# Attention and two expert layers on one core: the attention of a pair of heads written in two halves, with TensorE's instructions inside a half kept in the written order

## The chip, the core and the metric

The kernel runs on one core of a Trainium2 chip. The metric is device time in microseconds (us) for one launch, the median of several runs. Engines are named as in the profile: PE is TensorE's matmul stream, PEld its weight loads, DVE is VectorE, ACT is ScalarE, POOL is GpSimd, SP issues most DMAs.

## What is computed

Banded attention with four sink columns, then a dense gated layer, then a routed layer with one of eight experts per token, all in float32:

```python
# attention: 4 batches, 8 heads, 768 positions, head size 64, window 128, 4 sinks
scores = scale * np.matmul(q, k.transpose(0, 1, 3, 2))
keep = (pos[None, :] < n_sink) | ((rel >= 0) & (rel < window))
scores = np.where(keep, scores, -1e9); scores -= scores.max(-1, keepdims=True)
a = np.exp(scores); a = a / (a.sum(-1, keepdims=True) + 1e-9)
x = (a @ v).transpose(0, 2, 1, 3).reshape(3072, 512)
# dense layer: 512 -> 1024 (gated) -> 1024 -> 512
x = ((x @ w1) * (x @ w2)) @ w3 @ w_out
# routing and expert layer: 512 -> 1024 -> 512, one expert a token
logits = x @ w_gate + modality_bias[modality_id]
e_idx = argmax(logits); gate = softmax(logits)[e_idx]
out = gate * (relu(x @ e_w1[e_idx]) @ e_w2[e_idx])
```

## The kernel before

Precision comes from splitting: a float32 operand is held as a high and a low part, and a product is three matmuls (high by high, high by low, low by high). The weight product w3 @ w_out is formed once at the start (tiles `w3o`).

The tokens are cut into 12 units of 256 queries. One step of attention is a **pair** n: one unit and two heads, so there are 48 pairs, four to a unit. `att_stream` (L574) is a generator that traces the pairs; a pair is built of these functions:

- `a_scores(n, j)` (L441), for the two query blocks j = 0, 1: six matmuls at L458 into the tile `sp`, 64 rows of the array each (one head in the upper half, one in the lower). Then on DVE the mask (L470 or L475) and the row maximum (L484), on ACT the two exponentials (L486). `sp` has one buffer, so the scores of j = 1 wait for the exponentials of j = 0, and those of the next pair for the exponentials of j = 1. The normalisation on DVE (L491, L492, L497) is put off to a later step by `defer`.
- `a_pt(n)` (L518): four transposes of the probabilities at L527 into `pt`, a copy on ACT (L531), two masked copies on POOL (L536).
- `a_skT(n)` (L502): one or two transposes of the sink columns (L509).
- `a_pv(n)` (L541): the product with v at L555, 64 columns of the array each (one head left, one right), and the sinks' part at L558, then the split of the result into `xb` (L561 on ACT, L566 on DVE). The listing of the program shows four or six matmuls at L555 a pair; the trace has two records for each.
- `a_tqk(n)` (L389): from pair 8 on, the transposition of q and k on DVE (L407) and their split on ACT and DVE (L414 to L428).

The pairs are software pipelined: the step for pair n traces the scores of pair n, the transposes and the product with v of pair n - 1, and q and k of pair n + 1. `front` (L1014) mixes attention with the dense layer. For each of six groups of two units it runs `moe1_stream` (L687) and, between its pieces, as many steps of attention as a linear due time asks for (L1102, L1104). The dense layer of a group is eight pairs of products `ab` (L724, 24 matmuls of 512 columns per f), which DVE and ACT turn into `g`, `gh` and `gl` (L728 to L734, L701, L702), and the products `x2p` (L712) with `w3o`: first those of the first unit, mixed with `ab`, then, in the "late" part, those of the second unit alone. `route` (L775) follows: 16 multiply-and-sum instructions a unit on DVE (L785), a small ranking on PE (L807 to L811, tile `rk`), and the tables. `back` (L1126) then runs the expert layer (L933, L970).

What stands in the instruction queues is not the traced order. When the program is built, a scheduler reorders each engine's instructions: it goes through time by its own estimates and lets an engine take, of the instructions that it holds to be ready, the one with the best priority, which is the trace's order unless the code says otherwise. On the chip each engine's queue then runs strictly in the order so fixed, with semaphores between engines.

Of the kernel before, what the change touches and what calls it, by code (L numbers as in the profile page):

```python
# [27 lines left out]
def attention_moe_moe_kernel(ctx, tc, q, k, v, w1, w2, w3, w_out, mod_id, w_gate, mod_bias, e_w1, e_w2, out,  # L28
# [57 lines left out]
    def tick():  # L86
        for fn in waiting[0]:
            fn()
        waiting[0], waiting[1] = waiting[1], []

    def settle():
        while waiting[0] or waiting[1]:
# [253 lines left out]
    def a_load(n):  # L346
        u, p = divmod(n, NP)
        b, c = divmod(u, NC)
        hs = slice(2 * p, 2 * p + 2)
        qk = att.tile([128, 2, UNIT], F32, tag="qk", bufs=2, name="qk")  # L350
        for x, src in enumerate((q, k)):
            if n < BY_PE:
                for j in range(2):
                    s0 = c * UNIT + j * 128
                    nc.sync.dma_start(out=qk[:, x, j * 128:(j + 1) * 128].rearrange("p (h d) -> p h d", h=2),
                                      in_=src[b, hs, s0:s0 + 128, :].rearrange("h s d -> s h d"))
                continue
            for g in range(4):
                h, d0 = 2 * p + g // 2, g % 2 * 32
                nc.sync.dma_start(out=qk[g * 32:(g + 1) * 32, x].rearrange("p (b i) -> p b i", i=32),  # L360
                                  in_=src[b, h, c * UNIT:(c + 1) * UNIT, d0:d0 + 32].rearrange("(b s) i -> s b i", s=32))
        nat[n] = qk

    def a_load_v(n):
        u, p = divmod(n, NP)
        b, c = divmod(u, NC)
        hs = slice(2 * p, 2 * p + 2)
        vn = att.tile([128, 3, 2, D], F32, tag="vn", bufs=3, name="vn")
        for j in range(0 if c else 1, 3):
            s0 = c * UNIT + (j - 1) * 128  # L370
            nc.sync.dma_start(out=vn[:, j], in_=v[b, hs, s0:s0 + 128, :].rearrange("h s d -> s h d"))
        stt["v", n] = vn
        if n and c == 0 and p == 0:
            a_load_sinks(b)
# [143 lines left out]
    def a_pt(n):  # L518
        u, p = divmod(n, NP)
        b, c = divmod(u, NC)  # L520
        P = stt["p", n]
        for j in range(2):
            stt.pop(("norm", n, j))()
        tp = ps_t.tile([128, 4, 128], F32, tag="t", name="pt")
        for j in range(2):
            for h in range(2):
                nc.tensor.transpose(out=tp[:, 2 * j + h, :], in_=P[:, j, h * (KW + NS):h * (KW + NS) + 128], identity=idf)  # L527
        full = att.tile([128, 4, 128], F32, tag="ptf", bufs=1, name="ptf")
        parts = att.tile([128, 2, 2, 2, 128], F32, tag="ptp", bufs=1, name="ptp")
        i0 = 0 if c else 1  # L530
        nc.scalar.activation(out=full[:, 2 * i0:4], in_=tp[:, 2 * i0:4], func=ACTF.Copy)  # L531
        if i0:
            nc.scalar.activation(out=parts[:, 0, 0], in_=tp[:, 0:2], func=ACTF.Copy)
        for a, op in enumerate((ALU.is_ge, ALU.is_gt)):
            sign = 1 - 2 * a
            nc.gpsimd.affine_select(out=parts[:, a, i0:2].rearrange("p j h q -> p (j h) q"), in_=full[:, 2 * i0:4],  # L536
                                    pattern=[[0, 4 - 2 * i0], [sign, 128]], compare_op=op, fill=0.0, base=0,
                                    channel_multiplier=-sign)
        stt["pt", n] = parts
# [34 lines left out]
    def att_stream():  # L574
        a_tqk(0); yield
        a_load(1)
        a_load_sinks(0)
        a_vsink(0)
        yield
        for n in range(NN):  # L580
            if n + 2 < NN:
                a_load(n + 2)
            a_scores(n, 0); yield
            if n:
                a_load_v(n)
                a_pt(n - 1); a_skT(n - 1); yield
            if n + 1 < NN:
                a_tqk(n + 1)
            yield
            a_scores(n, 1); yield  # L590
            if n:
                a_pv(n - 1)
                att_done[0] = n
                if n % (NP * NC) == 0:
                    a_vsink(n // (NP * NC))
            yield
        a_pt(NN - 1); a_skT(NN - 1); yield
        a_pv(NN - 1)
        att_done[0] = NN
        yield  # L600
# [412 lines left out]

    def front():  # L1014
        att_it = att_stream() if banded else att_stream_full()
        steps = [0]

        def step_att():
            if next(att_it, 0) == 0:
                return False  # L1020
            steps[0] += 1
            tick()
            return True

        def att_upto(target):
            while steps[0] < target and step_att():
                pass

        unit_steps = ATT_STEPS * NP
        begun = 10 if banded else 4  # L1030
        wab_n = W_EARLY
        t = 0.0
        f64_ahead(2)
        if banded:
            a_load(0)
            a_load_v(0)
        f64_ahead(4)
        for i, c in enumerate(startup_stream()):
            t += c
            tick()  # L1040
            if att_done[0] < 2 * NP:
                att_upto(min(0.75 * (i + 1), 8) + 38 * t / 46700)
        early = []
        for gr in range(NU // 2):
            while att_done[0] < (2 * gr + 2) * NP:
                step_att()
            settle()
            last = gr == NU // 2 - 1
            if last:
                for _ in att_it:  # L1050
                    pass
                att_ctx.close()
                pool = p2a.enter_context(tc.tile_pool(name="p2a", bufs=1, side="right", reuse_waits="tile"))
                mem = mem_of(pool, wp, pool, pool, pool, pool, (ps_t, ps_ab, ps_x2, 1))
                p2a_pool.append(pool)
                mem["w1"] = halves(lambda: pool.tile([128, 1024], F32R, tag="w1", bufs=KD, name="w1"), mem["w"])
                rows0 = pool.tile([128, SLOT // 128, ROW], F32, name="xrows")
                t_banks = [mem["pt"], lambda: ps_x.tile([128, 512], F32, tag="x", name="x")]

                def next_bank():  # L1060
                    t_banks.reverse()
                    return t_banks[0]()

                mem["pt"] = next_bank

                def next_early(first=0):
                    slots.append(Slot(SLOT, (NU - 2 if slots else NU - 4) * UNIT, mem))
                    slots[-1].decide(first)

                def first_early():  # L1070
                    next_early(3)
                    slots[0].gather(rows0)

                first_early()
                early = [(10000 + 2000 * i, lambda i=i: slots[0].w1_piece(i)) for i in range(KD)]
                early += [(47000 + 1500 * i, next_early) for i in range(N_EARLY - 1)]
                early += [(57200 + 1300 * i, lambda i=i: slots[0].transposes(i)) for i in range(KD)]
            t, routed, s0 = 0.0, 0, steps[0]
            s1 = begun + (2 * gr + 3) * unit_steps
            for kind, c in moe1_stream(gr):  # L1080
                t += c
                tick()
                while gr == 0 and wab_n < KF and wab_n < W_EARLY + t / 4000:
                    wab_pair(wab_n)
                    wab_n += 1
                    if wab_n == KF:
                        wgate_by_expert()
                        start_ctx.close()
                        sp_[0] = m1_ctx.enter_context(tc.tile_pool(name="m1", bufs=1, reuse_waits="tile"))
                        consts_late()  # L1090
                        load_wgate()
                if last:
                    while early and t >= early[0][0]:
                        early.pop(0)[1]()
                    due = min(t, 46000) / 1100
                else:
                    due = min(t, 46000) / 1100
                while routed < due and kind != "late":
                    routed += 1
                    route_step()  # L1100
                if kind != "late":
                    att_upto(min(s0 + (s1 - s0) * t / 52000, s1))  # L1102
                else:
                    att_upto(s1 + unit_steps * (t - 52000) / 10400)  # L1104
            for _, fn in early:
                fn()
        settle()
# [131 lines left out]
```

## Time and profile before

| | |
|---|---|
| median of 3 runs | 975.77 us (975.64 to 976.39) |
| the profiled execution | 975.55 us |
| its span, first to last instruction | 973.8 us |
| PE busy | 932.9 us, 96% |
| DVE busy | 651.8 us, 67% |
| ACT busy | 440.5 us, 45% |
| POOL busy | 167.2 us, 17% |
| mean granted PE clock | 0.994 |

A busy time is the sum of the stretches in which an engine had an instruction in execution; consecutive matmuls overlap in the record (a 512-column matmul lasts about 0.39 us there and the next one starts 0.23 us after it), so what a matmul costs is read from the distance of two starts. A busy PE is not a PE at its best pace. The rows further down come from the views named above each of them.

### The profile page before, as it was taken

Reading aid. Unit: us, or ns where it says so; the run is one execution under the profiler, and the core shown is the slowest. Engines: PE = TensorE matmul, PEld = TensorE weight load, DVE = VectorE, ACT = ScalarE, POOL = GpSimd, SP = SyncE. Lnnn points to the kernel's source line nnn. Section 1 sums busy time; section 2 is a strip of 40 time slices with the busy share of each in tenths; the row PEclk is TensorE's granted clock in tenths of the full one; section 3 lists DMA queues with packets and bytes.
Section 4 is the critical chain, followed back from the end, with each engine's and each line's share of the span. In section 5 each row is a group of like instructions: output and inputs, shape, how many; then the busy total and the mean of one; then the engine's idle time right before and its main releaser. Section 6 shows DMA issues by size and latency. Waiting matters only on the chain. (4 is left out here: it accounts for less than half of the span.)

```text
span 973.8 us, 15418 instructions
## 1 busy us (share of the span) xinstructions
PE 932.9 (96%) x4840; PEld 709.7 (73%) x4840; DVE 651.8 (67%) x1953; ACT 440.5 (45%) x1218; POOL 167.2 (17%) x253
## 2 busy tenths in 40 slices
PE   4899999999999999999999999999999999999995
PEld 3567677767776777677767776887888888888883
DVE  7956996699659964896599649929934374333422
ACT  3687763454335433553365334314433443344433
POOL 1111121111112111211111112213021214111010
PEclk9999999999999999999999999999999999999998
DMA  8754754123212231236123200512446465443331
GB/s 258 237 149 122 210 121 127 34 53 71 51 23 48 61 56 20 52 71 44 23 53 67 56 9 9 178 40 87 139 164 129 153 69 191 132 149 120 109 134 41
DMA packets 168933, 94.02 MB, mean 97 GB/s; under 512 B 140231, under 2 KB 148679, under 8 KB 168720
## 3 DMA queue, kind: packets, MB, share of 16 engines
q1 hardware_dynamic: 164080, 80.13, 33.6%
q0 software_dynamic: 4768, 12.88, 4.1%
q8 instruction: 39, 0.64, 0.3%
q14 instruction: 46, 0.38, 0.2%
HBM read 80.14 MB, written 13.09 MB: 96 GB/s over the span
## 5 line engine op out<-in xcount | busy, mean ns | idle before, releaser
L724 PE MATMUL ab<-xb,wab 128*128 128x512 f32 x1152 | 288.7, 397 | 1.0 <-DVE g L734 1.0
L724 PEld LDWEIGHTS ab<-xb,wab 128*128 128x128 f32 x1152 | 209.7, 188 | 46.0 <-PE sp L458 1.1
L970 PE MATMUL x<-w 128*128 128x512 f32 x600 | 141.0, 392 | 0.0
L785 DVE CUSTOM_DVE_ANT_0 junk<-rows,wgb 128x512 bf16<-128x512 f32 x192 | 135.7, 707 | 2.0 <-ACT rows L772 0.9
L712 PE MATMUL x2p<-w3o,gh 128*128 128x512 f32 x384 | 128.9, 411 | 0.5 <-ACT gh L701 0.5
L970 PEld LDWEIGHTS x<-w 128*128 128x128 f32 x600 | 111.6, 188 | 23.1 <-DVE w L202 0.4
L536 POOL TENSOR_SCALAR_AFFINE_SELECT ptp<-ptf 128x512 f32<-128x512 f32 (+1 forms) x96 | 66.5, 716 | 308.0 <-ACT ptf L531 308.0
L701 ACT ACTIVATE gh<-g 128x256 fp32r<-128x256 f32 x96 | 39.9, 416 | 119.2 <-DVE g L731 98.6
L486 ACT ACTIVATE P<-sp,st 128x132 f32<-128x132 f32 (+1 forms) x192 | 69.2, 366 | 51.5 <-DVE st L484 45.8
L712 PEld LDWEIGHTS x2p<-w3o,gh 128*128 128x128 f32 x384 | 67.2, 188 | 18.0 <-ACT gh L701 2.9
L202 DVE TENSOR_TENSOR w<-wst,w 128x512 fp32r<-128x512 f32 x112 | 71.4, 685 | 10.5 <-ACT w L201 10.5
L937 DVE SCALAR_TENSOR_TENSOR w<-ab,w 128x512 fp32r<-128x512 f32 x48 | 33.1, 690 | 64.4 <-ACT w L936 64.2
L712 PE MATMUL x2p<-w3o,gl 128*128 128x512 f32 x192 | 76.0, 396 | 0.0
L933 PE MATMUL ab<-w,w 128*128 128x512 f32 x288 | 74.9, 395 | 0.0
L933 PE MATMUL ab<-w 128*128 128x512 f32 x288 | 73.6, 391 | 0.0
L201 ACT ACTIVATE w<-wst 128x512 fp32r<-128x512 f32 x112 | 63.4, 628 | 4.5 <-DMA wst<-in_moe_w_dram 4.5
L458 PE MATMUL sp<-ring,qh 64*128 64x264 f32 (+1 forms) x384 | 61.1, 329 | 3.2 <-ACT P L486 2.2
L458 PEld LDWEIGHTS sp<-ring,qh 64*128 64x128 f32 x384 | 37.0, 185 | 35.8 <-ACT P L486 15.5
L933 PEld LDWEIGHTS ab<-w,w 128*128 128x128 f32 x288 | 53.9, 188 | 12.4
L933 PEld LDWEIGHTS ab<-w 128*128 128x128 f32 x288 | 54.1, 188 | 12.1
L936 ACT ACTIVATE w<-ab 128x512 fp32r<-128x512 f32 x48 | 28.7, 597 | 71.8 <-PE ab L933 71.4
L974 POOL DMA_INDIRECT out_dram<-late,ti x25 | 25.2, 1009 | 203.9 <-ACT late L973 166.6
(201 smaller groups left out, 1392.9 us busy)
## 6 DMA issues: line engine op xcount, KB each, us to landing
wst<-in_moe_w_dram SPq DMA_DIRECT2D x56, 512.0 KB
f64st<-in_moe_w_dram SPq DMA_DIRECT2D x32, 512.0 KB
vn<-in_v_dram SPq DMA_DIRECT2D x128, 64.0 KB
xs<-rows SPq DMA_DIRECT2D x12, 513.0 KB
qk<-in_q_dram SPq DMA_DIRECT2D x160, 32.0 KB
qk<-in_k_dram SPq DMA_DIRECT2D x160, 32.0 KB
f64st<-in_moe_w_out_dram SPq DMA_DIRECT2D x8, 512.0 KB
wgb<-wgt SPq DMA_DIRECT2D x1, 2048.0 KB
```

What stands on the lines that cost most here:

```text
L201: nc.scalar.activation(out=hi, in_=src, func=ACTF.Copy)
L202: lo_eng.tensor_tensor(out=lo, in0=src, in1=f32(hi), op=ALU.subtract)
L458: nc.tensor.matmul(out=sp[:, h, c0:c0 + nk].rearrange("p (a b) -> p a b", b=KW), lhsT=a[hp, j, :], rhs=kr[hp, b_, blocks, c0:c0 + KW], sta ...
L486: nc.scalar.activation(out=rows[:, h], in_=seen[:, h], func=ACTF.Exp, bias=st[:, 0, h:h + 1], accum_out=st[:, 1, h:h + 1])
L536: nc.gpsimd.affine_select(out=parts[:, a, i0:2].rearrange("p j h q -> p (j h) q"), in_=full[:, 2 * i0:4], pattern=[[0, 4 - 2 * i0], [sign, ...
L701: nc.scalar.activation(out=gh, in_=g, func=ACTF.Copy)
L712: nc.tensor.matmul(out=x2p[t], lhsT=a[:, sl], rhs=b_, start=(f == 0 and i == 0), stop=(f == KF - 1 and i == 2))
L724: nc.tensor.matmul(out=bank[nm].rearrange("p (u t) -> p u t", u=2), lhsT=a, rhs=b_, start=(kk == 0 and i == 0), stop=(kk == KD - 1 and i = ...
L785: nc.vector.tensor_tensor_reduce(out=junk, in0=rows[:, t, 0:DM], in1=wgb[0][:, e, :], scale=1.0, scalar=0.0, op0=ALU.mult, op1=ALU.add, ac ...
L933: nc.tensor.matmul(out=hp, lhsT=a[:, fs], rhs=b_, start=(kk == 0 and i == 0), stop=(kk == KD - 1 and i == 2))
L937: nc.vector.scalar_tensor_tensor(out=h[:, 1], in0=hp, scalar=0.0, in1=f32(h[:, 0]), op0=ALU.max, op1=ALU.subtract)
L970: nc.tensor.matmul(out=op, lhsT=a[:, ts], rhs=b_, start=(f == 0 and i == 0), stop=(f == KF - 1 and i == 2))
```

## The change

The diff, with everything that it touches:

```diff
@@ -87,6 +87,21 @@
+    issued = [None]
+
+    def in_order(fn):
+        traced = nc.cur_bb.bb.instructions
+        first = len(traced)
+        got = fn()
+        for ins in traced[first:]:
+            if ins.engine == mybir.EngineType.PE:
+                if issued[0] is not None:
+                    tc.add_manual_dep(ins, issued[0], mybir.DependencyInfo(mybir.DependencyClass.NoSync,
+                                                                           mybir.DependencyReason.DATA), reason="in order")
+                issued[0] = ins.name
+        return got
@@ -580,6 +595,23 @@
         for n in range(NN):
             if n + 2 < NN:
                 a_load(n + 2)
+            if n > 2 * NP:
+                a_load_v(n)
+                issued[0] = None
+                in_order(lambda: (a_scores(n, 0), a_pt(n - 1), a_skT(n - 1)))
+                yield
+                if n + 1 < NN:
+                    a_tqk(n + 1)
+                yield
+                issued[0] = None
+                in_order(lambda: (a_scores(n, 1), a_pv(n - 1)))
+                att_done[0] = n
+                if n % (NP * NC) == 0:
+                    a_vsink(n // (NP * NC))
+                yield
+                yield
+                yield
+                continue
             a_scores(n, 0); yield
             if n:
                 a_load_v(n)
@@ -1014,9 +1046,10 @@
+        strict = [False]
...
-            if next(att_it, 0) == 0:
+            if (in_order(lambda: next(att_it, 0)) if strict[0] else next(att_it, 0)) == 0:
@@ -1077,7 +1110,13 @@
-            for kind, c in moe1_stream(gr):
+            strict[0] = False
+            moe_it = moe1_stream(gr)
+            while True:
+                piece = in_order(lambda: next(moe_it, None)) if strict[0] else next(moe_it, None)
+                if piece is None:
+                    break
+                kind, c = piece
```

From pair 9 on (`2 * NP` is 8) a pair is traced in two halves. The first holds the scores of block 0, the four transposes of the pair before and its sink transposes; the second the scores of block 1 and the product with v of the pair before. Inside a half each PE instruction gets an edge to the PE instruction traced before it. Such an edge binds the scheduler alone: no semaphore and no wait is added, and instructions of the dense layer may still be put between two of a half. A pair still takes five steps, two of them empty now, so the due times are those of before. The load of v moves ahead of the scores. `strict` is False throughout, so the two wrappers in `front` do what the lines did that they replace.

The instructions on every engine are the same in number and kind; their order is new. On PE the first row that differs lies at 118 us of the profiled execution, and from 629 us on the order is that of before. Two places follow. In the changed kernel's listing the line numbers are its own: L473 is L458 of before, L542 is L527, L524 is L509, L570 is L555, L573 is L558, L744 is L712.

First place, PE, about 290 us, in the late part of a group: the product with v of pair 20 (`xp<-ptp,vn` and the sinks' part `xp<-pskT_107,vsk`) among the products `x2p`, and behind it the scores of the next pair. Before:

```order
L555 MATMUL xp<-ptp,vn 64x256
L712 MATMUL x2p<-w3o,gh 128x512 x2
L712 MATMUL x2p<-w3o,gl 128x512
L555 MATMUL xp<-ptp,vn 64x256
L555 MATMUL xp<-ptp,vn 64x128 x3
L712 MATMUL x2p<-w3o,gh 128x512 x2
L712 MATMUL x2p<-w3o,gl 128x512
L555 MATMUL xp<-ptp,vn 64x128
L558 MATMUL xp<-pskT_107,vsk 128x256
L458 MATMUL sp<-ring,qh 128x264 x2
```

The same product with v in the changed kernel, with the scores of pair 21's second block ahead of it:

```order
L473 MATMUL sp<-ring,qh 128x264 x2
L473 MATMUL sp<-ring,ql 128x264 x2
L473 MATMUL sp<-ring,qh 128x264 x2
L570 MATMUL xp<-ptp,vn 64x256 x2
L570 MATMUL xp<-ptp,vn 64x128 x4
L573 MATMUL xp<-pskT_107,vsk 128x256
L744 MATMUL x2p<-w3o,gh 128x512 x2
```

The product, in three pieces before, is one piece now, and it stands directly behind a group of scores.

Second place, PE, just behind the first: the first half of pair 22 in the changed kernel, and the scores of its second block that follow.

```order
L473 MATMUL sp<-ring,qh 128x264
L744 MATMUL x2p<-w3o,gh 128x512 x2
L744 MATMUL x2p<-w3o,gl 128x512
L744 MATMUL x2p<-w3o,gh 128x512 x2
L744 MATMUL x2p<-w3o,gl 128x512
L473 MATMUL sp<-ring,qh 128x264
L473 MATMUL sp<-ring,ql 128x264 x2
L473 MATMUL sp<-ring,qh 128x264 x2
L542 MATMUL pt<-idf,P 128x128 x4
L524 MATMUL xp<-idf,P 8x128 x2
```

Behind these ten rows:

```order
L744 MATMUL x2p<-w3o,gh 128x512 x2
L744 MATMUL x2p<-w3o,gl 128x512
L744 MATMUL x2p<-w3o,gh 128x512 x2
L744 MATMUL x2p<-w3o,gl 128x512
L744 MATMUL x2p<-w3o,gh 128x512 x2
L473 MATMUL sp<-ring,qh 128x264 x2
```

The transposes stand directly behind the scores; this group of scores is cut after its first matmul, which no group of before was from 118 us on; and eight matmuls of `x2p` lie between the transposes and the next scores.

## Rows read from the trace of the kernel before

**Rows 1.** The page: busy time by engine, and PE's in 40 equal slices, in tenths.

```profile
PE 932.9 (96%) x4840; PEld 709.7 (73%) x4840; DVE 651.8 (67%) x1953; ACT 440.5 (45%) x1218; POOL 167.2 (17%) x253
...
PE   4899999999999999999999999999999999999995
```

**Rows 2.** Windows: stretch, its length, then busy us by engine, clock, DMA.

```profile
118.00:629.00 511.00, 500.38 (x2774) 367.61 (x2772) 398.40 (x1321) 234.36 (x750) 84.02 (x132) 1.00 0.30 58
191.00:226.00 35.00, 33.76 (x194) 22.62 (x193) 33.24 (x115) 21.35 (x74) 4.32 (x8) 1.00 0.27 49
286.00:327.00 41.00, 38.11 (x227) 25.97 (x226) 36.20 (x117) 22.53 (x74) 8.09 (x14) 1.00 0.23 41
...
252.00:286.00 34.00, 34.00 (x186) 26.21 (x185) 15.81 (x48) 11.87 (x36) 7.42 (x12) 1.00 0.24 44
```

**Rows 3.** Waits of PE, 118 to 629 us: us in total, times, longest.

```profile
PE pt L527 <- DVE P L497: 3.3, 5, 1.0
PE sp L458 <- ACT P L486: 1.8, 6, 0.5
```

**Rows 4.** Timeline of PE at 460 us: start, us recorded, line, names, shape, count.

```profile
460.36 2.89 PE L724 MATMUL ab<-xb,wab 128*128 128x512 f32 x12
463.09 0.60 PE L527 MATMUL pt<-idf,P 128*128 128x128 f32 x4
...
463.66 3.01 PE L724 MATMUL ab<-xb,wab 128*128 128x512 f32 x12
466.51 0.62 PE L712 MATMUL x2p<-w3o,gh 128*128 128x512 f32 x2
466.96 0.39 PE L712 MATMUL x2p<-w3o,gl 128*128 128x512 f32 x1
```

**Rows 5.** Timeline of PE at 148 us: scores alone, twelve `ab`, then v.

```profile
147.76 0.28 PE L458 MATMUL sp<-ring,qh 64*128 64x264 f32 x2
147.97 3.06 PE L724 MATMUL ab<-xb,wab 128*128 128x512 f32 x12
150.95 1.09 PE L555 MATMUL xp<-ptp,vn 128*64 128x256 f32 x12
```

**Rows 6.** Timeline of PE at 194 us: a product with v in two pieces.

```profile
193.84 0.39 PE L712 MATMUL x2p<-w3o,gl 128*128 128x512 f32 x1
194.16 0.65 PE L555 MATMUL xp<-ptp,vn 128*64 128x256 f32 x2
194.73 0.73 PE L712 MATMUL x2p<-w3o,gh 128*128 128x512 f32 x2
195.30 0.40 PE L712 MATMUL x2p<-w3o,gl 128*128 128x512 f32 x1
195.63 0.86 PE L555 MATMUL xp<-ptp,vn 128*64 128x256 f32 x6
196.42 0.33 PE L558 MATMUL xp<-pskT,vsk 96*128 96x128 f32 x1
```

**Rows 7.** Timeline of PE at 218 us: v whole, directly behind scores.

```profile
218.39 0.29 PE L458 MATMUL sp<-ring,qh 64*128 64x264 f32 x2
218.61 0.87 PE L555 MATMUL xp<-ptp,vn 128*64 128x256 f32 x8
219.41 0.33 PE L558 MATMUL xp<-pskT,vsk 96*128 96x128 f32 x1
```

**Rows 8.** Timeline of PE at 88 us: scores cut after their first matmul.

```profile
88.17 0.38 PE L458 MATMUL sp<-ring,qh 64*128 64x264 f32 x1
88.48 0.38 PE L563 MATMUL xp<-xb,neg_r 128*128 128x256 f32 x1
```

**Rows 9.** Timelines of PE, DVE and ACT, 214 to 218 us: from scores to exponentials.

```profile
214.33 0.28 PE L458 MATMUL sp<-ring,qh 64*128 64x264 f32 x2
...
215.37 0.42 DVE L475 COPY_PREDICATED sp<-cur_i,sp 128x256 f32<-128x256 int32 x1
...
217.79 0.20 ACT L486 ACTIVATION_READ_ACCUMULATOR P<-sp,st 128x1 f32 x1
```

## The prediction

> **What bounds the kernel now.** I read the page first. PE is busy for 932.9 us of a span of 973.8, and its 40 slices are nines from the third to the last but one [rows 1]. So a PE that never starves sets the time, and what counts is the pace at which it takes instructions, which a busy share hides. Next come the windows of the stretch in which the change moves anything, 118 to 629 us: PE has something in execution for 500.38 of 511 us at a clock of 1.00, so only 10.6 us are open waits [rows 2]. Behind 629 us PE's order is unchanged and its slices are full, so whatever is won or lost before shifts the rest as a whole; of the rest I expect nothing of its own.
>
> The same windows show that the stretch is of two kinds. In a light part, 252 to 286 us, DVE works 15.81 of 34 us. In a dense part, the late part of a group, 191 to 226 us, it works 33.24 of 35 us, and 36.20 of 41 between 286 and 327 [rows 2]. There are five dense parts, one per group from the first to the fifth; the one at 484 us repeats that at 191. There DVE is nearly as much of a bound as PE. The waits of PE say the same: the largest are transposes for normalised probabilities, 3.3 us in 5 waits, and scores for the exponentials that free `sp`, 1.8 us in 6 [rows 3].
>
> Last, the timeline, for the price of attention's small matmuls among the large ones. Twelve `ab` in a row take 463.09 - 460.36 = 2.73 us. The same twelve behind transposes take 466.51 - 463.66 = 2.85, so leaving a group of transposes costs 0.12 [rows 4]. Scores occupy half the array's rows (64*128), the product with v half its columns (128*64). Going into one of them costs as well: two `x2p` before another take 0.45 us, so one takes 0.225 [rows 4], but one before a product with v takes 194.16 - 193.84 = 0.32, an entry price of 0.09; and two behind it take 195.30 - 194.73 = 0.57, an exit price of 0.12 [rows 6]. PE loses time per visit of attention, not only per matmul.
>
> **The change, part by part.** No instruction is added or removed, and an edge for the scheduler is not a wait, so its own price is nothing. What changes is how often PE goes to and fro. I counted, over PE's whole listing between 118 and 629 us, the runs of attention matmuls (lines 458, 509, 527, 555, 558) that stand between large ones: 171 before, 115 now. By kind:
>
> 1. *Products with v cut in pieces*: 53 pieces for 41 products before, 41 pieces now, so 12 cuts go, all in dense parts. The two records of the first piece take 194.73 - 194.16 = 0.57 us, and the six of the second 0.79; all eight in one piece take 219.41 - 218.61 = 0.80 [rows 6, 7]. The cut thus costs 0.56, and with a second entry and exit (0.09 + 0.12) 0.77. Some pieces stand beside scores and save the second entry, so I take 0.65 between these ends: 12 x 0.65 = 7.8 us saved, 6.7 to 9.2.
> 2. *A product with v directly behind scores*: 7 before, 32 now. Scores, twelve `ab` and the product apart: the twelve take 150.95 - 147.97 = 2.98 us, 0.25 above the plain 2.73 [rows 4, 5]. Joined, the product starts 218.61 - 218.39 = 0.22 us behind the last scores, where `ab` starts 147.97 - 147.76 = 0.21 behind them, and it is no longer than elsewhere [rows 5, 7]. So a join saves an entry and an exit, 0.21 by their prices, 0.25 by the row. I take 0.21: 25 x 0.21 = 5.2 us saved.
> 3. *Transposes directly behind scores*: 9 before, 35 now. One exit goes and one stays; no row here shows what the passage itself costs, so the gain is between 0 and 0.16 (0.25 - 0.09). I take 0.06, half an exit, for lack of a nearer row: 26 x 0.06 = 1.6 us, 0 to 4.2.
> 4. *Scores cut after their first matmul*: none before in the stretch, 5 now, one at the head of each dense part. At 88 us such a cut stands: the lone matmul takes 88.48 - 88.17 = 0.31 us [rows 8], and the next entry 0.09. That is 5 x 0.4 = 2.0 us lost.
>
> Together 7.8 + 5.2 + 1.6 - 2.0 = 12.6 us less for PE.
>
> *What takes some of it back.* All of item 1 and about half of item 2 lie in dense parts, and item 4 does: 1.6 + 0.5 - 0.4 = 1.7 us each. The dense part at 191 us has only 35 - 33.24 = 1.76 us in which DVE is idle [rows 2], and DVE's work, the 16 multiply-and-sums of a unit's routing among it, is the same. DVE cannot lose all its idle time, since it waits for PE too. In the two dense parts of this kind I let half the gain go to new waits of PE for DVE, 0.85 each, and 0.25 in each of the other three, where 41 - 36.20 = 4.8 us are left at the largest: 1.7 + 0.75, about 2.4 us. Waits that DVE and ACT cause today I leave at their 10.6 us, between 0 and the doubling that rival D makes of them.
>
> *What moves on the queues at no cost.* The loads of v are issued one step earlier on SP. They keep their three buffers, and the DMA share is 0.27 to 0.30 in the dense part and over the stretch [rows 2]. If that cover were gone, the product with v would be late, which stands behind scores now, so that the next scores would be late with it. The two empty steps issue nothing.
>
> The sum: -12.6 + 2.4 = -10.2 us. Against the profiled execution's 975.55 us that is 965.4; the median of the runs lies 0.2 above that execution, so the forecast is **965.6 us**. A measurement of this kernel can tell about 0.2% (2 us) from no change.
>
> **Rivals.**
>
> *A. The waits shrink too.* The transposes of a pair now stand behind the next pair's first scores, so the normalisation has longer. For it: PE's largest wait is just that one. Against: in the dense parts DVE, which does the normalisation, is full. If both listed waits went, 3.3 + 1.8 = 5.1 us [rows 3], the time would be 960.5.
>
> *B. DVE is the bound in all dense parts.* They keep their length, and 5 x 1.7 = 8.5 us of the 12.6 are lost instead of 2.4. For it: 33.24 of 35. Against: 36.20 of 41 in the longest. The time would be 965.6 + 6.1 = 971.7.
>
> *C. A join saves nothing.* If PE had to empty itself between scores and product too, as these use the array differently, item 2 would drop out: 965.6 + 5.2 = 970.8. Against it stand the 0.22 us and the unchanged 0.80 [rows 7]; only seven joins exist in the trace, so I do not exclude it. The Trainium skill speaks for this rival: TensorEngine Tiling (Array Packing), section Tiling Modes, says that a change of the tiling mode, not merely of the tile, drains the engine, and 64*128 and 128*64 are two modes. By that rule the joins would be worth nothing; the trace agrees with it for the entry from 128*128 (0.09) but does not show it between the two.
>
> *D. Slower: the bunched halves wait at their head.* The scores of the second block wait for the exponentials of the first. In the dense part at 214 us the last scores start at 214.33, DVE reaches the mask at 215.37 behind its routing work, and the last read-out of the exponentials ends at 217.79 + 0.20 = 217.99: 3.66 us [rows 9]. In the new order of pair 22 six transposes (463.66 - 463.09 = 0.57 [rows 4]), eight `x2p` (8 x 0.225 = 1.8), the 0.21 behind the scores and an exit and entry (0.21) lie between, some 2.8 us. Behind the waiting scores now stands the whole product with v. A wait of 0.85 in each of the 20 pairs of the dense parts (four in each) is 17 us: 975.8 - 12.6 + 17 = 980.2. It decides from 12.6 / 20 = 0.63 us per pair on. Against: these scores already wait today (the 1.8 us), 3.66 is a pair with a busy DVE, and a PE that waits there lets DVE catch up, so that the next pair waits less.
>
> *E. It comes out even.* New waits eat between 80% and 120% of the 12.6 us; the time stays within 2 us of 975.8. That the change does not do what it says is excluded for the order itself, which the listing shows; that the order matters is what the entry and exit prices say.
>
> **How the numbers follow.** The forecast's own band, 961.5 to 969.5, gets 0.56; A 0.11, B 0.13, C 0.04, E 0.09, D 0.07. Faster by over 0.2%: 0.56 + 0.11 + 0.13 + 0.04 = 0.84. Same: 0.09. Slower: 0.07. The range holds A down to 959.5 and B and C up to 973; outside remain E, D and a tail of A, not quite 2 in 10. The bounds of items 1 to 3 (6.7 to 9.2, 5.2 to 6.2, 0 to 4.2) lie inside.
>
> **What the next profile would show.** Right: the stretch to the unchanged part ends near 619 us instead of 629; products with v in one piece at 0.8 to 1.02 us, each 0.22 behind scores; the dense parts one to three microseconds shorter with DVE still nearer to full; PE waiting mainly for ACT at scores and for DVE at transposes, some 13 us in all. Wrong: a joined product that is longer or later than 0.22 (C); dense parts of old length with DVE full (B); PE's waits for the exponentials many times 1.8 us (D). I would be wrong altogether if the expert layer behind 629 us did not shift with the rest, say because its first weights or tables came later.

## The result and the profile after

The changed kernel takes **965.69 us** (965.21 to 966.02, 4 runs) against 975.87 for the kernel before in the same runs (975.64 to 976.39): a ratio of 0.9895, 95% interval 0.9877 to 0.9912. The forecast was 965.6, so the time lies where it was put; whether for the reasons given is what the rest is about.

Busy times and PE's slices of the changed kernel, from the page, answer to [rows 1]:

```profile
PE 922.2 (96%) x4840; PEld 711.4 (74%) x4840; DVE 650.6 (68%) x1953; ACT 439.3 (46%) x1218; POOL 169.0 (18%) x253
...
PE   4899999999999999999999999999999999999994
```

PE's busy time fell by 10.7 us with the same 4840 matmuls and the same share of 96%. The page alone cannot say more. To compare like with like, I cut each trace at the same two matmuls, the 541st and the 3331st in PE's order: the changed orders lie between them and PE's listing is the same outside. The windows of that stretch (length; then busy us of PE, PEld, DVE, ACT and POOL; then clock and DMA), before:

```profile
116.26:630.42 514.16, 503.54 (x2792) 370.23 (x2791) 401.45 (x1333) 235.63 (x754) 86.81 (x135) 1.00 0.30 60
...
190.31:225.84 35.53, 34.29 (x196) 23.03 (x195) 33.34 (x115) 21.19 (x74) 4.16 (x7) 1.00 0.26 48
286.48:326.60 40.12, 37.23 (x224) 25.25 (x223) 36.13 (x117) 22.46 (x74) 8.09 (x14) 1.00 0.23 42
...
251.86:286.48 34.62, 34.62 (x188) 26.72 (x187) 15.81 (x48) 11.87 (x36) 7.56 (x12) 1.00 0.23 43
```

and after, with the same four stretches (whole, two dense parts, one light part, each from the end of one `ab` product to that of another):

```profile
116.73:620.27 503.54, 492.76 (x2792) 371.94 (x2791) 400.19 (x1330) 233.97 (x752) 86.43 (x133) 1.00 0.31 60
...
190.46:224.16 33.70, 32.16 (x191) 22.73 (x190) 32.24 (x109) 19.53 (x68) 3.74 (x6) 1.00 0.26 48
284.43:322.24 37.81, 35.50 (x224) 24.80 (x223) 35.43 (x113) 22.09 (x73) 8.24 (x14) 1.00 0.25 44
...
250.40:284.43 34.03, 34.03 (x189) 26.88 (x187) 15.28 (x52) 11.64 (x36) 7.07 (x10) 1.00 0.30 44
```

The stretch is 10.6 us shorter. PE's busy time in it fell by 503.54 - 492.76 = 10.8 us; what PE stood idle went from 514.16 - 503.54 = 10.62 to 10.78 us. So the whole gain is pace, and the waits are as long as before. The two dense parts shown lost 1.83 and 2.31 us, the light one 0.59; all five dense parts together went from 180.9 to 172.1 us. Not all of these 8.8 us were saved there: the second dense part holds the same attention work in both kernels, but the first, third and fourth each hold 48 matmuls of the scores instead of 54, so one group of six has moved out of each. In the first DVE was idle for 2.19 us and is now for 1.46. The rest of the program moved as a whole: behind the 3331st matmul 330.9 us pass to the last one in both. Ahead of the stretch the changed execution was 0.47 us later (116.73 against 116.26), so its whole span is shorter by 10.0 us (973.8 to 963.8) and not by 10.6.

The waits of PE between 118 and 619 us after, answering to [rows 3]:

```profile
PE pt L542 <- DVE P L512: 3.7, 6, 1.0
PE sp L473 <- ACT P L501: 2.2, 8, 0.6
```

They are a little longer than the 3.3 and 1.8 of before. Last, PE's timeline about 285 us, the place of the listings above (start, recorded us):

```profile
285.08 0.29 PE L473 MATMUL sp<-ring,qh 64*128 64x264 f32 x2
285.30 1.09 PE L570 MATMUL xp<-ptp,vn 128*64 128x256 f32 x12
286.31 0.39 PE L573 MATMUL xp<-pskT,vsk 96*128 96x256 f32 x1
286.54 0.62 PE L744 MATMUL x2p<-w3o,gh 128*128 128x512 f32 x2
...
288.58 0.62 PE L744 MATMUL x2p<-w3o,gh 128*128 128x512 f32 x2
289.04 0.39 PE L744 MATMUL x2p<-w3o,gl 128*128 128x512 f32 x1
289.35 0.39 PE L473 MATMUL sp<-ring,qh 64*128 64x264 f32 x1
289.67 0.73 PE L744 MATMUL x2p<-w3o,gh 128*128 128x512 f32 x2
290.24 0.39 PE L744 MATMUL x2p<-w3o,gl 128*128 128x512 f32 x1
```

The product with v starts 0.22 us behind the last scores and runs in one piece of 1.01 us. The cut group of scores shows its price whole: 0.31 from `gl` to the lone matmul instead of 0.225, 0.32 for the matmul, and 0.57 for the two `x2p` behind it instead of 0.45 [rows 4].

### The profile page after: what moved, and what is told of

It reads as the page before. It is cut to its first block, busy times and chain, and to the rows that moved or that the text cites. A ratio compares the mean times of both kernels' runs of the same rounds, so it can differ in the third digit from the quotient of the medians.

```text
span 963.8 us, 15412 instructions
## 1 busy us (share of the span) xinstructions
PE 922.2 (96%) x4840; PEld 711.4 (74%) x4840; DVE 650.6 (68%) x1953; ACT 439.3 (46%) x1218; POOL 169.0 (18%) x253
## 5 line engine op out<-in xcount | busy, mean ns | idle before, releaser
L756 PE MATMUL ab<-xb,wab 128*128 128x512 f32 x1152 | 279.5, 393 | 0.1
L756 PEld LDWEIGHTS ab<-xb,wab 128*128 128x128 f32 x1152 | 212.8, 188 | 44.4 <-DVE xb L581 0.5
L744 PE MATMUL x2p<-w3o,gh 128*128 128x512 f32 x384 | 126.7, 405 | 0.4 <-ACT gh L733 0.4
L744 PEld LDWEIGHTS x2p<-w3o,gh 128*128 128x128 f32 x384 | 68.2, 188 | 13.9 <-ACT gh L733 1.1
L744 PE MATMUL x2p<-w3o,gl 128*128 128x512 f32 x192 | 75.9, 395 | 0.0
L763 DVE TENSOR_TENSOR g<-ab,bs 128x256 f32<-128x256 f32 x48 | 20.2, 420 | 79.7 <-PE ab L756 55.0
L473 PEld LDWEIGHTS sp<-ring,qh 64*128 64x128 f32 x384 | 37.9, 184 | 38.1 <-ACT P L501 15.9
L473 PE MATMUL sp<-ring,qh 64*128 64x264 f32 (+1 forms) x384 | 62.7, 328 | 3.1 <-ACT P L501 2.4
L965 PEld LDWEIGHTS ab<-w 128*128 128x128 f32 x288 | 54.1, 188 | 12.1
```

The costliest lines, as they stand in the source:

```text
L473: nc.tensor.matmul(out=sp[:, h, c0:c0 + nk].rearrange("p (a b) -> p a b", b=KW), lhsT=a[hp, j, :], rhs=kr[hp, b_, blocks, c0:c0 + KW], sta ...
L744: nc.tensor.matmul(out=x2p[t], lhsT=a[:, sl], rhs=b_, start=(f == 0 and i == 0), stop=(f == KF - 1 and i == 2))
L756: nc.tensor.matmul(out=bank[nm].rearrange("p (u t) -> p u t", u=2), lhsT=a, rhs=b_, start=(kk == 0 and i == 0), stop=(kk == KD - 1 and i = ...
L965: nc.tensor.matmul(out=hp, lhsT=a[:, fs], rhs=b_, start=(kk == 0 and i == 0), stop=(kk == KD - 1 and i == 2))
```

## The experiments

My theory was the prediction's: PE pays for every entry into and every exit out of a group of matmuls that use part of the array, so cuts cost (0.65 us for a product with v, 0.4 for scores) and joins of scores and product save (0.21). Its rivals: the edges or the waits are what counts; the joins save nothing; DVE is the bound in the dense parts. Three questions had to be told apart, and twelve kernels ran. For each I cut the trace at the same two matmuls; all numbers of these windows stand in one table behind the last run.

**Tracing or edges?** The change does two things at once. The first run keeps the halves and leaves the edges out:

```diff
-                in_order(lambda: (a_scores(n, 0), a_pt(n - 1), a_skT(n - 1)))
+                a_scores(n, 0); a_pt(n - 1); a_skT(n - 1)
...
-                in_order(lambda: (a_scores(n, 1), a_pv(n - 1)))
+                a_scores(n, 1); a_pv(n - 1)
```

> The two halves are traced as in the change, but no edge is added. TensorE's listing between 118 and 629 us then has 45 pieces of products with v instead of 41, 29 products directly behind scores instead of 32, 26 transposes behind scores instead of 35. Theory (the time follows the number of entries and exits): 4 x 0.65 + 3 x 0.21 + 9 x 0.06 = 3.8 us back of the 10.2, so about 969.5 us. Rival 1 (the edges are the whole gain): 975.8. Rival 2 (the tracing in halves is the whole gain, the edges do nothing): 965.7.

Measured: 965.2 us (ratio 0.9893, 0.9878 to 0.9908), the time of the change. The theory's 969.5 missed and the second rival's 965.7 came. The window says that it is still not that rival's plain story:

```profile
116.90:620.00 503.10, 494.75 (x2792) 371.74 (x2791) 398.94 (x1329) 235.54 (x753) 86.00 (x135) 1.00 0.30 61
```

PE is busy 2.0 us longer than in the change, where the prices say 3.8 for what the edges spare, and idle for 8.35 us instead of 10.78. The edges buy pace and pay for it in waits. The four cuts that are left have the scores of the next pair between the two pieces of a product, and no large matmul:

```profile
200.57 0.62 PE L570 MATMUL xp<-ptp,vn 128*64 128x256 f32 x2 [0.55 <-POOL ptp L551]
201.12 0.39 PE L473 MATMUL sp<-ring,qh 64*128 64x264 f32 x2
...
201.68 0.86 PE L570 MATMUL xp<-ptp,vn 128*64 128x256 f32 x6
```

The second run keeps the five steps and has edges alone (the lines added to the kernel before):

```diff
+            if n > 2 * NP:
+                issued[0] = None
+                in_order(lambda: a_scores(n, 0)); yield
+                a_load_v(n)
+                issued[0] = None
+                in_order(lambda: (a_pt(n - 1), a_skT(n - 1))); yield
...
+                in_order(lambda: a_scores(n, 1)); yield
+                issued[0] = None
+                in_order(lambda: a_pv(n - 1))
```

> Edges alone: the five steps of before, each with its own chain of edges inside the step, from pair 9 on. The listing has 52 pieces of products with v (53 before, 41 in the change), 7 directly behind scores, 6 transposes behind scores. Theory (entries and exits): nearly nothing is left of the gain, about 975 us, within 1 us of before. Rival (an edge within a step is enough): 966.

Measured: 976.63 us (ratio 1.0011, 1.0002 to 1.0020). Edges within the old steps bring nothing.

**Do joins pay?** The third run takes the second half apart into two steps, each with its own chain:

```diff
-                in_order(lambda: (a_scores(n, 1), a_pv(n - 1)))
+                in_order(lambda: a_scores(n, 1)); yield
+                issued[0] = None
+                in_order(lambda: a_pv(n - 1))
```

> The first half as in the change; the scores of block 1 and the product with v in two steps, each with its own chain, so that they are seldom joined: 11 joins instead of 32, 44 pieces of products with v instead of 41. Theory (a join saves an entry and an exit, 0.21 us): 21 x 0.21 + 3 x 0.65 = 6.4 us more than the change, 972.1 us. Rival (TensorE empties itself between the two forms anyway, a join saves nothing): 3 x 0.65 = 2.0 us more, 967.7 us.

Measured: 970.74 us (ratio 0.9950, 0.9936 to 0.9963), 5.1 us above the change; PE's busy time rose by 5.7 and its idle time fell by 0.5. That is near the 6.4 of the theory and far from the 2.0 of a join that saves nothing.

The fifth and sixth runs trace one half alone as one step, without edges (the other half keeps its steps). The fifth, against the change:

```diff
+                a_scores(n, 0); yield
                 a_load_v(n)
-                issued[0] = None
-                in_order(lambda: (a_scores(n, 0), a_pt(n - 1), a_skT(n - 1)))
-                yield
+                a_pt(n - 1); a_skT(n - 1); yield
...
-                in_order(lambda: (a_scores(n, 1), a_pv(n - 1)))
+                a_scores(n, 1); a_pv(n - 1)
```

> Only the second half is traced as one step (scores of block 1 and the product with v), without edges; the first half keeps the steps of before. Listing: 44 pieces of products with v (53 before), 30 directly behind scores (7), 8 transposes behind scores (9), 5 groups of scores cut (0). Theory (cuts and joins pay, by the prices on record): 9 x 0.65 + 23 x 0.21 - 5 x 0.4 = 8.7 us saved, about 967 us. Rival (each half brings half of the gain, whatever the joins): about 970.7 us.

> Only the first half is traced as one step (scores of block 0, transposes), without edges; scores of block 1 and the product with v are two steps. Listing: 45 pieces of products with v, 10 directly behind scores, 26 transposes behind scores, 5 groups of scores cut. Theory (cuts and joins): 8 x 0.65 + 3 x 0.21 + 17 x 0.06 - 5 x 0.4 = 4.8 us saved, about 971 us. Rival (transposes behind scores are what pays): 966 us; rival (each half brings half of the gain): 970.7 us, which this run alone does not tell from the theory.

Measured: 970.42 us (ratio 0.9943, 0.9929 to 0.9957) and 969.61 (0.9935, 0.9921 to 0.9948). By the times, half of the gain each, as the rival had it. PE's busy time goes with the theory: the second half saves 8.1 us of the 8.7 expected and loses 2.4 again in waits, mostly of the product with v for POOL's masked copies (6.4 us in 9 waits where before had 0.3 in one); the first half saves 4.1 of 4.8 and has 2.3 us less of waits. The times agreed with the rival because the waits happened to lie so; no count on record gives these waits.

The seventh run turns the second half round:

```diff
-                in_order(lambda: (a_scores(n, 1), a_pv(n - 1)))
+                in_order(lambda: (a_pv(n - 1), a_scores(n, 1)))
```

> The change with the second half turned round: the product with v and the sinks' part first, then the scores of block 1, in one chain of edges. Listing: 41 pieces of products with v, none behind scores; the scores stand behind the sinks' part instead, which occupies 96 rows. Theory (a join pays between scores and product because nothing of another height lies between; behind the sinks' part the entry is paid anew): 32 x 0.21 = 6.7 us of the gain go, about 972.5 us. Rival (fewer visits are what pays, in whatever order): 111 visits against 115, 965 to 966 us.

Measured: 980.12 us (ratio 1.0036, 1.0023 to 1.0050), slower than before, and far from the rival: fewer visits are not what pays. But it is 7.6 us above the theory too. PE's busy time is 13.9 us above the change's instead of 6.7 (the trace is of an execution of 981.99 us). The timeline and the windows of that kernel show why:

```profile
134.44 1.15 PE L570 MATMUL xp<-ptp,vn 128*64 128x256 f32 x12 [2.11 <-POOL wgst L790]
...
136.99 5.40 PE L756 MATMUL ab<-xb,wab 128*128 128x512 f32 x12
142.23 0.64 PE L744 MATMUL x2p<-w3o,gh 128*128 128x512 f32 x2
...
257.11 0.39 PE L573 MATMUL xp<-pskT,vsk 96*128 96x256 f32 x1
257.43 0.40 PE L473 MATMUL sp<-ring,qh 64*128 64x264 f32 x2
```

```profile
131.00:135.20 4.20, 2.09 (x16) 1.46 (x16) 4.14 (x10) 2.26 (x5) 2.86 (x3) 1.00 0.62 94
135.20:142.00 6.80, 6.80 (x25) 5.04 (x22) 6.23 (x15) 2.43 (x8) 0.00 (x0) 0.51 0.34 63
...
469.70:476.50 6.80, 6.80 (x27) 5.05 (x24) 4.14 (x12) 2.55 (x8) 0.21 (x2) 0.51 0.21 41
```

The scores start 257.43 - 257.11 = 0.32 us behind the sinks' part, where `x2p` in the change starts 286.54 - 286.31 = 0.23 behind the same matmul: 0.09 more, an entry, is paid there, as expected. And twice PE waited for over 2 us in front of a product with v, after which the granted clock stood at 0.51 (1.2 instead of 2.4 GHz) for 6.8 us; twelve `ab` took 142.23 - 136.99 = 5.24 us there and 2.73 at the full clock [rows 4]. Half of the time at half clock, 2 x 3.4 = 6.8 us, is an estimate of what this cost, and 13.9 - 6.8 = 7.1 is near the theory's 6.7.

**Do cuts cost?** The eighth run makes more of them, by giving both halves ten places of priority:

```diff
-                in_order(lambda: (a_scores(n, 0), a_pt(n - 1), a_skT(n - 1)))
+                with tc.high_priority(offset=10):
+                    in_order(lambda: (a_scores(n, 0), a_pt(n - 1), a_skT(n - 1)))
...
-                in_order(lambda: (a_scores(n, 1), a_pv(n - 1)))
+                with tc.high_priority(offset=10):
+                    in_order(lambda: (a_scores(n, 1), a_pv(n - 1)))
```

> The change with the instructions of each half raised in priority by 10 places, which makes the scheduler cut far more: 355 visits instead of 115, 130 pieces of products with v instead of 41, 143 pieces of scores instead of 84. Theory (a cut costs TensorE time each): 89 x 0.65 + 59 x 0.4 = 81 us more, about 1047 us; at least 89 x 0.56 + 59 x 0.3 = 68 us more. Rival (the cuts cost nothing, the gain came from waits): within 10 us of the change.

Measured: 1048.26 us (ratio 1.0751, 1.0728 to 1.0775). PE's busy time is 78.1 us above the change's (74.7 without an estimated 3.4 for a clock at half), of 81 expected, its idle time 1.3. The run makes cuts of both kinds at once, so it bears out their sum and not each price. The timeline shows what such a stretch looks like:

```profile
252.28 0.39 PE L473 MATMUL sp<-ring,qh 64*128 64x264 f32 x1
252.60 0.50 PE L758 MATMUL ab<-xb,wab 128*128 128x512 f32 x1
253.03 0.39 PE L473 MATMUL sp<-ring,qh 64*128 64x264 f32 x1
253.34 0.50 PE L758 MATMUL ab<-xb,wab 128*128 128x512 f32 x1
253.77 0.38 PE L473 MATMUL sp<-ring,ql 64*128 64x264 f32 x1
```

Each lone matmul of the scores takes 0.31 to 0.32 us and each lone `ab` 0.43 instead of 0.23, with nothing waiting: PE reads as fully busy.

**Is DVE the bound in the dense parts?** The fourth run takes the routing's work out of them. Every DVE instruction of a routing step gets an edge to the gating product traced last before it:

```diff
+            last_g[0] = [i_.name for i_ in nc.cur_bb.bb.instructions[seen_:] if i_.engine == mybir.EngineType.DVE][-1]
...
+            for ins in nc.cur_bb.bb.instructions[seen_:]:
+                if ins.engine == mybir.EngineType.DVE and last_g[0] is not None:
+                    tc.add_manual_dep(ins, last_g[0], mybir.DependencyInfo(mybir.DependencyClass.NoSync,
+                                                                           mybir.DependencyReason.DATA), reason="routing later")
```

> The change, and each routing step's VectorE instructions are bound by edges behind the gating product that was traced last before them. The multiply-and-sums that VectorE runs in the dense part of a group fall from 17 to 23 to 3, the others move to the light part. Theory (in the dense parts a full VectorE delays masks and normalisations, and TensorE waits): TensorE's waits there, some 8 us over the five dense parts above the pace without waits, mostly go, and 14 fewer visits save another 2 us: about 957 us. Rival 1 (the chain from scores to exponentials is long by itself): the dense parts stay as they are, 964 to 966 us. Rival 2 (the light parts now wait instead): 966 to 970 us.

Measured: 966.34 us (ratio 0.9912, 0.9899 to 0.9926). No gain; the theory, 957, fell, and the time lies at the border of the two rivals. Two dense parts and a light one of this kernel, cut as above:

```profile
192.68:228.65 35.97, 34.43 (x210) 24.27 (x209) 27.12 (x85) 21.98 (x78) 3.69 (x8) 1.00 0.29 54
287.45:324.87 37.42, 35.29 (x224) 25.13 (x223) 28.67 (x86) 22.72 (x77) 5.42 (x14) 1.00 0.27 48
...
253.39:287.45 34.06, 34.06 (x189) 26.87 (x188) 26.46 (x93) 11.88 (x37) 7.72 (x10) 1.00 0.25 59
```

DVE is now idle for 8.8 us in each of the two dense parts (24%), and PE still stands idle 1.54 us in the first and 2.13 in the second, where the change has 1.54 and 2.31. Over all five dense parts PE's idle time is 6.8 us against 7.5. (The first holds 19 more matmuls than in the change, so its length is not compared.) So DVE was full there with routing work that could lie elsewhere, and PE's idle time there hardly hung on it. Over the whole stretch the two waits of [rows 3] did fall, from 5.9 to 3.4 us, but the wait list shows new ones in their place, 3.6 us for the ranking:

```profile
PE rk L841 <- DVE oh L830: 2.1, 4, 0.6
PE pt L542 <- DVE P L512: 1.9, 5, 0.7
PE rk L841 <- DVE rows L837: 1.5, 1, 1.5
PE sp L473 <- ACT P L501: 1.5, 7, 0.4
```

No run moves the routing later and spares the ranking its wait, so it is open whether the two together would gain.

**Which half's edges bring the waits?** Two runs have the edges in one half only, two more combine this with the later routing. The edits are those above, each in one place.

> The change with edges in the second half alone (scores of block 1 and product with v); the first half is traced as one step without edges. Listing: 41 pieces of products with v, as in the change (45 without any edges). Between the same two matmuls TensorE had 492.8 us busy and 10.8 idle in the change, 494.8 and 8.4 without edges. Theory (the edges of the second half spare four cuts, those of the first half bring the waits): 492.8 busy and 8.4 idle, 2 us less than either, about 963.4 us. Rival (the edges of the second half bring the waits themselves): about 965.5 us.

> The change with edges in the first half alone (scores of block 0 and transposes). Listing: 44 pieces of products with v, 35 transposes behind scores. Theory (these edges bring the waits and spare no cut): 494.5 busy and 10.8 idle, about 967.3 us. Rival (the edges of the second half bring the waits): about 965.2 us.

> Edges in the second half alone, and the routing steps bound behind the gating products as in the earlier run with later routing. Theory (waits of the first half's edges gone, VectorE freer in the dense parts, the waits for the ranking stay): 2.4 us less than that run's 966.3, about 964 us. Rival (no such waits were there once routing is later): 966.

> No edges for attention, halves as in the change, routing later. Listing: 47 pieces of products with v, 36 directly behind scores. Theory (6 more cuts than the run with edges and later routing, 0.5 us each; waits 2.4 us fewer): about 967 us. Rival (cuts no longer cost where VectorE has room): about 964 us.

Measured: 964.19 us (ratio 0.9881, 0.9867 to 0.9895), 966.36 (0.9903, 0.9888 to 0.9917), 968.29 (0.9926, 0.9908 to 0.9944) and 971.34 (0.9955, 0.9936 to 0.9974). By their times the first two lie between theory and rival; by the windows they went the theory's way: edges in the second half have the change's busy time to the hundredth (492.76) and 1.6 us fewer waits, edges in the first half 493.9 us busy and 10.4 idle, of 494.5 and 10.8 expected. 964.19 is the lowest time of the study, but its interval overlaps the change's, so it is not shown to be the better kernel. The last two missed. Their executions lie in two groups, 966.5 to 966.9 and 969.7 to 972.6 us in the eleventh run and 968.5 to 969.4 and 973.3 to 974.6 in the twelfth, and both traces are of the upper group; what the lower group spares is not shown. In the twelfth run's trace the waits are not where I looked; its lists for PE and, from 376 to 392 us, for DVE:

```profile
PE x2p L744 <- ACT gh L733: 2.4, 1, 2.4
...
DVE qk L422 <- DMA qk<-in_k_dram: 7.9, 1, 7.9
```

DVE stood 7.9 us before a load of k and everything behind it was late; the wait of PE was followed by a clock at half here too (0.56 on the mean from 388.0 to 391.5 us). Why that load came late with later routing was not tried.

The table sets all runs beside the prices on record: pieces of products with v, pieces of scores, products behind scores, transposes behind scores as counted in the listing; the change of PE's busy time against before that the prices give (0.65, 0.4, 0.21, 0.06 each) and that the windows show; and PE's idle time.

| run | v | scores | joins | transposes | prices | busy measured | idle | time |
|---|---|---|---|---|---|---|---|---|
| before | 53 | 79 | 7 | 9 | | | 10.6 | 975.87 |
| the change | 41 | 84 | 32 | 35 | -12.6 | -10.8 | 10.8 | 965.69 |
| 1 halves, no edges | 45 | 84 | 29 | 26 | -8.8 | -8.8 | 8.4 | 965.2 |
| 2 old steps, edges | 52 | 79 | 7 | 6 | -0.5 | -0.3 | 11.7 | 976.63 |
| 3 second half apart | 44 | 84 | 11 | 35 | -6.2 | -5.1 | 10.3 | 970.74 |
| 4 routing later | 41 | 84 | 37 | 35 | -13.7 | -11.0 | 12.3 | 966.34 |
| 5 second half only | 44 | 84 | 30 | 8 | -8.6 | -8.1 | 13.0 | 970.42 |
| 6 first half only | 45 | 84 | 10 | 26 | -4.8 | -4.1 | 8.3 | 969.61 |
| 7 v before scores | 41 | 87 | 0 | 36 | -4.7 | -3.7 | 13.8 | 980.12 |
| 8 many cuts | 130 | 143 | 28 | 32 | +69.9 | +63.9 | 12.1 | 1048.26 |
| 9 edges second half | 41 | 84 | 31 | 26 | -11.9 | -10.8 | 9.2 | 964.19 |
| 10 edges first half | 44 | 84 | 30 | 35 | -10.2 | -9.6 | 10.4 | 966.36 |
| 11 as 9, routing later | 41 | 84 | 37 | 34 | -13.6 | -12.8 | 16.2 | 968.29 |
| 12 as 1, routing later | 47 | 84 | 36 | 32 | -9.4 | -9.7 | 15.7 | 971.34 |

From the measured values of runs 7, 8, 11 and 12 half of the time at half clock is taken off (6.8, 3.4, 3.4 and 1.7 us; 3.07, 67.34, -9.41 and -7.97 without that); this is an estimate. Each window is of one execution: those of runs 4, 7, 8, 11 and 12 took 968.95, 981.99, 1044.92, 972.33 and 973.3 us, while the last column has medians. Busy times span 78 us, and the prices meet them within 10% at the far end and within 2.7 us elsewhere, or within 1.7 us if transposes are priced at nothing; the idle times, between 8 and 16 us, follow no count of mine.

## Why the prediction came out right

*The bound.* PE's pace with PE busy throughout, and the shift of all that follows: right. The stretch shrank by 10.6 us, the remainder kept its 330.9.

*Items 1 and 2, cuts and joins: right.* Products are in one piece, 0.22 us behind the scores, as in [rows 7]; the third and seventh runs moved mostly joins, the eighth mostly cuts, and the busy time followed. The price of one cut is less sure. The ninth run has four cuts fewer and two joins more than the first and is busy 1.99 us less, so those four, by scores, cost about (1.99 - 2 x 0.21) / 4 = 0.4 us each and not 0.65; four of the twelve of item 1 are of this kind. Item 2 was weighed against the Trainium skill's rule (TensorEngine Tiling (Array Packing), Tiling Modes) that a change of tiling mode drains the engine. By the rule a join would be worth nothing. The traces agree with it between 128*128 and either partial form (0.09 in, 0.12 out) and from the sinks' part, 96*128, to 64*128 (0.09), and do not show it from 64*128 to 128*64, where the measurement decides. Rival C fell with that.

*Items 3 and 4: mis-sized, by little.* For transposes I took half an exit for lack of a row. The ninth run against the change singles them out: it has nine transposes fewer directly behind scores and one join fewer, the other counts equal, and the same 492.76 us busy. So item 3 is worth nothing that shows, where I had 1.6 us. The cut of scores was read from a place where no large matmul followed [rows 8], so I left out the exit of 0.12 that the change's timeline shows: 5 x 0.53 = 2.6 us instead of 2.0. These two move the sum from -12.6 to -10.4, near the measured -10.8; with the four cuts of item 1 at 0.4 it would be -9.4, so how the gain divides among the items stays an estimate.

*What takes some of it back: wrong.* I let 2.4 us go to new waits for DVE. The idle time grew by 0.16, and the fourth run, with a quarter of the two dense parts shown free on DVE, had nearly the same idle time in them. The step that failed is reading 33.24 of 35 us [rows 2] as a need; a good part of it was routing work that could lie elsewhere. An error of 1.8 us in the gain and one of 2.2 in the loss cancelled, and the 0.4 us left over went against the 0.47 us ahead of the stretch, so that 965.6 agrees so closely with 965.69 is luck.

*The split by place* comes out nearer than the lengths say: I expected 6 us from the dense parts, and they are 8.8 shorter, but three groups of scores have left them. At 201.68 - 201.12 = 0.56 us a group in company, or 0.77 with an entry and an exit, that is 1.7 to 2.3 us, and an estimate of 6.5 to 7.1 remains.

*Rivals.* A did not come (the two listed waits grew from 5.1 to 5.9 us), B fell with the second dense part, 2.31 us shorter with the same attention work, and with the fourth run; D's wait exists (2.2 us in 8 waits) but is far below the 0.63 a pair from which it decides. E fell. What none of them had: the edges, which give the change its name, are not needed. The tracing in halves brings the gain alone (first run), the edges nothing without it (second).

## What to carry to other kernels

Where TensorE reads as busy throughout, as with the 96% here, read its pace: compare the distance of two starts inside a run of equal matmuls with that at the borders of runs, and count the borders in the order. In this kernel matmuls that use part of the array were cheap in company and dear alone: one of the scores took 0.32 us between two `ab`, and two at the end of a group 0.22. So keep a group whole, and try which forms can stand side by side: the product with v behind scores saved an entry and an exit, scores behind the sinks' part or transposes behind scores saved nothing that showed. An engine that reads as full can be filled with work that could lie elsewhere: take the work away before believing it a bound.

## What had not been expected

Edges traded cuts for waits almost one to one: 2.0 us of busy time saved for 2.4 us of idle time (first run against the change), and the waits came mostly with the edges of the first half (10.4 us idle against 9.2 with those of the second).

A wait of PE can cost twice. Behind waits of 2.1 and 2.2 us in the seventh run, of 2.4 in the eighth and the twelfth and of 2.8 in the eleventh the clock was at half (1.2 instead of 2.4 GHz) for 6.8, 6.8, 3.4, 3.4 and 6.8 us; in the change, whose longest wait in the stretch is 1.4 us, it was not. In the seventh run that made an estimated 6.8 of the 16.4 us between its profiled execution and the change's. But the clock also fell once where PE had not waited, in the eighth run, behind lone matmuls of the scores and lone `ab` in turn, as in the lines from 252 us above:

```profile
423.00:426.40 3.40, 3.40 (x11) 1.73 (x11) 0.20 (x1) 0.00 (x0) 0.00 (x0) 1.00 0.00 0
426.40:429.80 3.40, 3.40 (x7) 1.06 (x6) 2.23 (x8) 1.53 (x6) 0.00 (x0) 0.50 0.00 0
```

PE reads as busy from 412 us to the fall. Those lines at 252 us were not followed by it, so whether the cuts brought it is not shown.
